# One core, attention and MLP: the scheduler's priorities replaced by an explicit sequence, and w_in loaded by column quarters

## The chip, the cores and the metric

The kernel runs on one core of a Trainium2 chip. The metric is the device time of one execution in microseconds (us), smaller is better. Executions of one kernel scatter by some 1%. "Before" is the kernel without the change, "the changed kernel" the one with it.

Engines: PE is TensorE (PEld its weight loads), DVE VectorE, ACT ScalarE, POOL GpSimd, SP SyncE, which here only issues DMAs.

## The reference, cut to what matters

Block-sparse attention (every query keeps the 6 best of 24 key chunks of 32, chosen by an upper bound), then an MLP with hard-swish:

```python
B, H, S, D = 4, 8, 768, 64
ub = sum(maximum(q * k_min, q * k_max))             # per query and chunk
top_chunks = argsort(ub)[..., -6:]                   # causal chunks only
scores = where(selected & causal, q @ k.T / 8, -1e9)
x = (softmax(scores) @ v) -> [3072, 512]
h = x @ w_in                                         # 512 -> 2048
out = (h * clip(h + 3, 0, 6) / 6) @ w_out            # 2048 -> 512
```

## The kernel before: the parts that the change and the argument touch

Two heads make a "pair"; there are 16 pairs, four to a batch. The kernel does not emit its instructions in source order. It first lists all its parts as `Op`s with an engine, a duration, a key (smaller is sooner), dependencies and ring buffers, then a list scheduler goes through them in modelled time and emits them. For a pair i the parts are, in the naming that I use throughout: k, q, v (loads), C (V cast on POOL), K and Q (transposes on PE, then copies and minima and maxima), R (Q copy in bf16 on POOL), U, V, L (bound, top 6, selection), S.0 to S.5 (score bins; exponential on ACT, mask on POOL), P (attention times V). For a group g of 384 tokens: X (transposes), H.0 to H.14 (eight groups of 8 matmuls, then ACT and DVE), O (output, in quarters of 4 matmuls). w0 to w3 load w_in, w4 to w7 w_out.

```python
def run(self, slack):
    ...                                        # cut: candidates, dependencies
            for eng, lst in cand.items():
                mine = None
                for op in lst:
                    if op.key is None:
                        op.key = front
                    r = self.ready(op)         # None while its ring buffer is in use
                    ...
                    if mine is None or (at + s < mine[0]) or (at < mine[0] + s and op.key < mine[1].key):
                        mine = (at, op)

rings = dict(big=3, sm=2, ks=3, qs=3, vb=3, vs=3, ...)       # buffers; big and sm are PSUM

s["ldk"] = add("LD", 2.07, i - 4.0, lambda: ld(s["ks"], k, "KS"), take=[s["ks"]], chain="ldk")
s["ldq"] = add("LD", 2.07, i - 3.9, lambda: ld(s["qs"], q, "QS"), take=[s["qs"]], chain="ldq")

for kt in range(KT_HID):                       # w_in by row blocks, issued from POOL (they cast to bf16)
    iss = add("POOL", 0.6, 0.3 + 0.05 * kt,
              lambda kt=kt: nc.gpsimd.dma_start(WIN[:, kt, :], moe_w_in[kt * P:(kt + 1) * P, :]),
              deps=[st[2 + kt // 2]["o_v"]], chain="wi")
    res.append(add("LD", 3.1, 0.01 * kt, None, deps=[iss], chain="w"))

ORDER = "K3 S0 L1 P0 Q3 S1 P1 S2 U2 S3 V2 S4 S5".split()     # one pair's keys; the MLP gets a pace
```

The plan models DMA: one lane "LD", one load after the other by key, and the weights (`None` as their function) in the same lane. On the chip the weight loads go through a queue of their own (q0 in the DMA views below) and land some 8 us after POOL issues them (median 8.6 us for w_in, 8.0 for w_out).

The softmax here doesn't subtract the row's maximum and nothing guards it: scores larger than these inputs give would overflow.

## Time and profile before

| | before |
|---|---|
| time | 320.94 us, median of 3 runs (320.07 to 321.49) |
| span of the profiled execution | 321.6 us (that execution took 323.29 us) |
| PE busy | 296.4 us, 92% |
| DVE, ACT, POOL busy | 174.0, 178.9, 76.8 us |
| chain of waits | 85% PE |
| first H matmul | 67.4 us |

From the page of the kernel before: busy time, then the granted PE clock and the DMA rate in 40 slices of 8 us.

```profile
PE 296.4 (92%) x2976; PEld 177.1 (55%) x2992; DVE 174.0 (54%) x464; ACT 178.9 (56%) x217; POOL 76.8 (24%) x149
...
PEclk9769977999999999999999999999999999999999
DMA  9998999997606144361401200000011001100101
GB/s 211 265 242 177 211 202 202 195 229 171 147 9 141 67 101 113 82 153 30 101 34 67 49 2 35 33 35 2 2 45 56 0 3 65 35 0 35 65 33 65
```

The reader is to see three things. PE is the busiest engine by far. The clock is granted below full speed only in the first seven slices. And DMA is busy for 70% or more of each of the first ten slices, partly used in the next ten, and nearly idle after that.

From the chain of waits of the kernel before (start, duration, engine, tile, line), up to L of pair 3:

```profile
34.54 0.56 DVE Xb L462
35.10 0.88 DVE KM L283
35.97 0.02 issue
36.00 0.81 ACT LHS L298
36.80 0.02 issue
36.83 0.96 DVE KC_122 L283
37.79 0.10 DVE RINV L457
37.89 0.74 DVE QP L313
38.62 0.71 DVE KC_122 L291
39.34 1.08 DVE T_654 L362 x12
40.41 0.46 DVE Xb L462
40.87 0.38 DVE SEL_127 L365
41.24 0.05 issue
41.29 0.30 PE SLT L382 x3
```

Here the chain leaves PE for 7 us. It does so again ahead of the next two L (47.8 to 51.5 and 55.8 to 60.5 us), for 3.7 and 4.8 us. What PE waits for is the selection, which stands behind other work in DVE's order. This is what a better order can shorten.

The loads of Q for pair 7 in the kernel before (all DMAs that write QS in 46 to 52 us):

```profile
L243 SPq DMA_DIRECT2D QS<-in_q_dram x2: 627/1823/3019, 46.6 to 49.7; - x2
...
DMA to landing us min/median/max: 8.7/9.9/11.1
```

PE used them at 65.8 us, just ahead of its first five H groups:

```profile
65.81 0.83 PE L273 MATMUL QT<-IDENT_111,QS 128*128 128x128 f32 x6
...
67.44 6.67 PE L514 MATMUL HP<-XT,WIN 128*128 128x384 bf16 x40
```

### The profile page before, as it was taken

To read this page: it belongs to the slowest core of one execution; us is meant where nothing else is said; L and a number is where in the kernel's file an instruction comes from. 1 tells how busy PE (TensorE), PEld (TensorE's weight loads), DVE (VectorE), ACT (ScalarE), POOL (GpSimd) and SP (SyncE) were. 2 spreads that over 40 slices of the span, in tenths; PEclk is the share of its full clock that TensorE was granted. 3 is DMA by queue.
4 is the path that set the end of the run, shared out by engine and by line. 5 is a ranking of instruction groups with operands and counts; after the bars stand their busy time and mean duration, and the time that the engine had idled before them with its cause. 6 is when DMAs were issued, how large, how long until landed. Compare 5 with 4: busy or idle time off the path is not lost.

```text
span 321.6 us, 7243 instructions
## 1 busy us (share of the span) xinstructions
PE 296.4 (92%) x2976; PEld 177.1 (55%) x2992; DVE 174.0 (54%) x464; ACT 178.9 (56%) x217; POOL 76.8 (24%) x149
## 2 busy tenths in 40 slices
PE   3567888899999999999999999999999999999995
PEld 2345665666665464576546564566555555564542
DVE  7367955789786052478534683466522541471330
ACT  0428856866876154666656665586455862462431
POOL 7125654721431012140322122240211211000000
PEclk9769977999999999999999999999999999999999
DMA  9998999997606144361401200000011001100101
GB/s 211 265 242 177 211 202 202 195 229 171 147 9 141 67 101 113 82 153 30 101 34 67 49 2 35 33 35 2 2 45 56 0 3 65 35 0 35 65 33 65
DMA packets 81440, 29.82 MB, mean 93 GB/s; under 512 B 75776, under 2 KB 77824, under 8 KB 81408
## 3 DMA queue, kind: packets, MB, share of 16 engines
q1 hardware_dynamic: 77152, 24.78, 31.2%
q0 software_dynamic: 2688, 4.19, 7.7%
q10 hardware_dynamic: 1568, 0.39, 0.5%
q8 instruction: 23, 0.38, 0.5%
q14 instruction: 9, 0.07, 0.1%
HBM read 27.26 MB, written 6.29 MB: 104 GB/s over the span
## 4 chain that ended last, share of the span: by engine, by line
PE 85%; DVE 8%; ACT 4%; issue 1%; POOL 1%; POOLq 0%; ACTq 0%
PE HP L514 26%; PE OP L538 26%; PE SPS L412 7%; PE PVP L452 7%; PE SPS L417 5%; PE KT L273 4%; PE UBP L332 3%; PE QT L273 2%; PE XTP L494 2%; PE UBQ L354 2%; DVE KM L283 1%; ACT U L518 1%; PE SLT L382 1%; DVE EM L230 1%; ACT LHS L298 1%
## 5 line engine op out<-in xcount | busy, mean ns | idle before, releaser
L423 ACT ACTIVATE PT<-SPS 128x1024 bf16<-128x1024 f32 x96 | 85.3, 919 | 38.8 <-PE SPS L417 37.8
L514 PE MATMUL HP<-XT,WIN 128*128 128x384 bf16 x512 | 89.5, 326 | 1.2 <-DVE GT L524 1.2
L538 PE MATMUL OP<-WOUT,GT 128*128 128x512 bf16 x368 | 86.5, 380 | 1.5 <-issue 1.0
L524 DVE SCALAR_TENSOR_TENSOR GT<-U,HP 128x768 bf16<-128x768 bf16 x64 | 60.9, 952 | 40.0 <-ACT U L518 39.8
L518 ACT ACTIVATE U<-HP,THREE 128x768 bf16<-128x768 f32 x64 | 57.7, 901 | 37.9 <-PE HP L514 37.3
L427 POOL TENSOR_SCALAR_AFFINE_SELECT PT<-PT 128x256 bf16<-128x256 bf16 x96 | 39.1, 413 | 127.2 <-ACT PT L423 125.1
L514 PEld LDWEIGHTS <-WIN 128*128 128x128 bf16 x512 | 47.9, 98 | 33.0 <-issue 3.7
L538 PEld LDWEIGHTS <-GT 128*128 128x128 bf16 x384 | 35.2, 98 | 42.5 <-issue 4.0
L412 PE MATMUL SPS<-RHS,LHS 64*128 64x512 bf16 (+3 forms) x256 | 35.8, 318 | 2.5 <-ACT PT L423 1.9
L544 ACT ACTIVATE OT<-OP 128x512 f32<-128x512 f32 x24 | 14.3, 596 | 41.2 <-PE OP L538 39.0
L417 PE MATMUL SPS<-SELT,EM 64*128 64x288 bf16 (+6 forms) x384 | 33.4, 255 | 0.0
L452 PEld LDWEIGHTS <-PT 128*128 128x128 bf16 x672 | 24.8, 101 | 3.6 <-issue 2.0
L283 DVE TENSOR_REDUCE KM<-KT 128x24 f32<-128x768 f32 x16 | 15.3, 954 | 17.4 <-PE KT L273 17.0
L412 PEld LDWEIGHTS <-LHS 64*128 64x128 bf16 x256 | 11.4, 95 | 21.7 <-issue 18.3
L417 PEld LDWEIGHTS <-EM 64*128 64x128 bf16 x384 | 19.0, 97 | 7.8 <-issue 1.4
L319 POOL CAST RHS<-QTS 128x768 bf16<-128x768 f32 x16 | 14.7, 920 | 33.2 <-ACT QTS L309 28.3
L273 PE MATMUL KT<-IDENT_111,KS 128*128 128x128 f32 x96 | 16.2, 313 | 4.2 <-DMA KS<-in_k_dram 4.2
L298 ACT CAST LHS<-KT 128x768 bf16<-128x768 f32 x16 | 12.8, 799 | 12.0 <-DVE KM L283 8.6
L462 DVE TENSOR_TENSOR Xb<-PVP,RINV 128x384 bf16<-128x384 f32 x32 | 17.6, 554 | 0.8
L457 DVE RECIPROCAL RINV<-PVP 128x6 f32<-128x6 f32 x32 | 6.1, 192 | 22.0 <-PE PVP L452 21.9
L340 DVE TENSOR_TENSOR UBT<-UBP,BIAS 96x384 f32<-96x384 f32 x16 | 8.8, 549 | 16.1 <-PE UBP L332 16.1
L313 DVE TENSOR_SCALAR QP<-QTS 128x576 f32<-128x576 f32 x16 | 11.3, 705 | 10.0 <-ACT QTS L309 9.9
(103 smaller groups left out, 229.6 us busy)
## 6 DMA issues: line engine op xcount, KB each, us to landing
VS<-in_v_dram SPq DMA_DIRECT2D x32, 192.0 KB, 3.6
out_dram<-OT SPq DMA_DIRECT2D x24, 256.0 KB, 2.0
KS<-in_k_dram SPq DMA_DIRECT2D x31, 192.0 KB, 3.3
QS<-in_q_dram SPq DMA_DIRECT2D x31, 192.0 KB, 3.5
WIN<-in_moe_w_in_dram POOLq DMA_DIRECT2D x4, 512.0 KB, 8.6
WOUT<-in_moe_w_out_dram POOLq DMA_DIRECT2D x4, 512.0 KB, 8.0
KS<-in_k_dram ACTq DMA_DIRECT2D x1, 192.0 KB, 3.3
QS<-in_q_dram ACTq DMA_DIRECT2D x1, 192.0 KB, 4.4
```

The source lines that it names most:

```text
L273: nc.tensor.transpose(T[:, j * P:(j + 1) * P], src.obj[:, j].rearrange("p e d -> p (e d)"), IDENT32[:])
L283: nc.vector.tensor_reduce(out=dst, in_=kt.obj[:, 0:S].rearrange("p (c w) -> p c w", w=CH), axis=AX.X, op=op)
L412: nc.tensor.matmul(T[:, e, c:c + hi - lo], lhsT=s["lhs"].obj[e * D:(e + 1) * D, j * P:(j + 1) * P], rhs=s["rhs"].obj[e * D:(e + 1) * D, lo ...
L417: nc.tensor.matmul(T[:, e, c:c + hi - lo], lhsT=EM[e * D:(e + 1) * D, h, j * P:(j + 1) * P], rhs=s["selt"].obj[e * D:(e + 1) * D, x:x + hi ...
L423: nc.scalar.activation(T[:, :, 0:w], sp.obj[:, :, 0:w], ACT.Exp, scale=scale)
L427: nc.gpsimd.affine_select(out=dv, in_=dv, pattern=[[0, 2], [1, P]], compare_op=A.is_ge, fill=0.0, base=0, channel_multiplier=-1)
L452: nc.tensor.matmul(T[:, qb, :], lhsT=t[:, e, c:c + P], rhs=fx(s["vb"])[:, e, j, :], start=(j == 0), stop=(j == qb))
L462: nc.vector.tensor_tensor(out=xb[b].obj[:, :, h * D:(h + 1) * D], in0=pv.obj[:, :, 0:D], in1=s[("ri", e)][:].to_broadcast([P, NBLK, D]), o ...
L514: nc.tensor.matmul(T[:, f, 0:GRP], lhsT=WIN[:, kt, (f0 + f) * P:(f0 + f + 1) * P], rhs=xt.obj[:, kt, :], start=(kt == 0), stop=(kt == KT_H ...
L518: nc.scalar.activation(new(u, [P, 2, GRP], BF16, "U")[:], hp.obj[:, :, 0:GRP], ACT.Relu, bias=THREE[:], scale=1.0)
L524: nc.vector.scalar_tensor_tensor(out=gt.obj[:, f0:f0 + 2, :], in0=u.obj[:], scalar=6.0, in1=hp.obj[:, :, 0:GRP], op0=A.min, op1=A.mult)
L538: nc.tensor.matmul(T[:, :], lhsT=gt.obj[:, f, t * P:(t + 1) * P], rhs=WOUT[:, f, :], start=(f == 0), stop=(f == FT - 1))
```

## The change

Intent: take the order of all parts from one explicit sequence, found by annealing in the plan's own model, with durations set closer to the measured ones; and load w_in by column quarters, so that H.0 needs one quarter of it and not all.

```diff
-    def add(self, eng, dur, key, fn=None, deps=(), take=(), use=(), chain=None):
+    def add(self, eng, dur, tok, fn=None, deps=(), take=(), use=(), chain=None):
...
-        op = Op(eng, dur, key, fn, deps, take, use)
+        op = Op(eng, dur, tok, self.place(tok), fn, deps, take, use)
...
+SEQUENCE = """
+V0 S0.2 R0 K0 k2 q1 R3 w7 q0 S0.4 S0.1 U0 k3 v5 v0 R1 P0.0 v6 w4 S3.0 R2 S0.0 v1 S0.3 S0.5 V2 V4 k0 w0 k4 w6 Q3
...                                      (some 30 lines)
+POS = {tok: n for n, tok in enumerate(SEQUENCE.split())}
...
-        for kt in range(KT_HID):
-            iss = add("POOL", 0.6, 0.3 + 0.05 * kt,
-                      lambda kt=kt: nc.gpsimd.dma_start(WIN[:, kt, :], moe_w_in[kt * P:(kt + 1) * P, :]),
-                      deps=[st[2 + kt // 2]["o_v"]], chain="wi")
+        for n in range(4):
+            c = n * (DFF // 4)
+            iss = add("POOL", 0.63, f"w{n}",
+                      lambda c=c: nc.gpsimd.dma_start(WIN[:, :, c:c + DFF // 4], wi[:, :, c:c + DFF // 4]),
+                      deps=[st[WGATE[n]]["o_v"]], chain="wi")
...
-            o = add("PE", 1.30, kk, mm, deps=xts + wdma[:KT_HID], take=[hp], use=[xt], chain="H")
+            o = add("PE", 1.31, tok, mm, deps=xts + [wdma[f0 * 4 // FT]], take=[hp], use=[xt], chain="H")
...
-    ORDER = "K3 S0 L1 P0 Q3 S1 P1 S2 U2 S3 V2 S4 S5".split()
```

The order that PE gets around the first H (built, not run): `... S4.0 X0.0 U5 X0.2 U6 V5 H0.0 Q7 V6 L5 S4.1 H0.2 H0.4 ...`. Before, five H groups ran at the first opportunity and Q7 came just ahead of them.

## The prediction

> **What bounds the kernel now.** TensorE, but not evenly. The page gives PE 296.4 us busy of 321.6 (92%), the others 56% or less; the chain of waits is 85% PE. Priced from warm pieces of the chain: one H group (8 matmuls of 384) 1.30 us, an O quarter 0.86, a P 0.66, a K or Q transpose group 0.66, U 0.80, V 0.47, L 0.30, X 0.33, the S bins of a pair about 2.7. Times their counts, the program is about 281 us at full clock. About 40 us are lost:
>
> - Front. In the chain the first H matmul starts at 67.5 us. What ran before it (PE timeline: K, Q of pairs 0 to 7, U 0 to 6, V 0 to 5, S, P of 0 to 3) is an estimated 38 us of full-clock work, so about 30 us are lost. In the busy-by-stretch view PE is idle 11.6 us in 0-24 us and 6.2 us in 24-64, and the granted clock is 0.79, 0.62, 0.79, 0.79 in 8-16, 16-24, 40-48, 48-56. (The Trainium skill, "TensorE: Matmul & The Clock Gate", part 1, says an under-used PE is clocked at half rate in windows of about 3.4 us; the clock row agrees.) The chain there is not PE: from 34.3 to 41.2 and 47.8 to 51.5 us it runs through DVE and ACT (KM, KC, QP, T8, SEL), ending in SLTs that PE waited for, 0.7 to 1.3 us. A pair takes 9 to 10 us, while its work is some 7 us on each of PE, ACT and DVE.
> - Middle, 67.5 to 318 us: about 7 us, around H groups mixed with S and P (gaps near 97-103 and 178-186 us).
> - End: 3.5 us, the last output copy and store.
>
> **What the change does.** Same arithmetic; it only reorders. The built order keeps the first eight PE groups (K0 to U1) and the load order of pairs 0 to 8. Then: all six S0 bins in one run; K3 before P0 and U4, V4 before S3, so selection runs further ahead of the S that needs it; most of S4 before the first H; H in runs of mostly seven or eight; K7, K8, K9 put under O work; O5.2 between the last P and the last X's. Before the first H stands an estimated 37-38 us of PE work, as before, so an earlier first H is pure gain.
>
> w_in by column quarters: same bytes, 2 KB source rows instead of 8 KB. w_out's pieces already have 2 KB rows and land in 8.0 us against 8.6, so no cost. H then needs one quarter, but w_in wasn't the wait: first H follows P3 and X0 closely.
>
> **Sum.** Up to S0 at 20.5 us nothing changes. From there ACT (exponentials 1.02 us, copies 0.8) with three PSUM buffers sets the pace; walking the order I get S1 near 31, S2 near 39, first H at 59-63 instead of 67.5: 6 to 8 us gained. Middle: 2 to 5 us. End: 0. Predicted 310 us, range 302 to 317. Chances: faster by over 2% 0.73, within 2% 0.25, slower 0.02.
>
> **Right if:** first H near 61 us; PE idle after 24 us roughly halved; granted clock about 1.00 from 32 us on; PE busy falls to about 290; busy time of DVE, ACT, POOL unchanged; S0 still starts near 20.5.
>
> **Wrong if:** runs of S and K bunch on ACT or DVE, which work strictly in order, so that real waits exceed the plan's; faster consumption meets the DMA limit (about 200 GB/s throughout 0-72 us now) and K or Q loads come late; half clock moves elsewhere. More gain if the front reaches ACT's bound, first H near 55.

## The result, and the profile after

Ratios here and below are the mean time of one kernel's fast runs over the mean of the other's of the same rounds, so not quite the ratio of the medians that are quoted.

| | before | changed |
|---|---|---|
| median time | 321.19 us (4 runs) | 315.82 us (4 runs, 315.66 to 317.32) |
| ratio | | 0.985, 95% interval 0.9811 to 0.9888 |
| PE busy | 296.4 us | 292.0 us |
| span, profiled | 321.6 us | 314.1 us |
| first H | 67.4 us | 60.4 us |

So 1.5% faster, which counts as the same at a 2% line; 3.4% had been forecast. From the page of the changed kernel:

```profile
PE 292.0 (93%) x2992; PEld 178.4 (57%) x2992; DVE 173.8 (55%) x464; ACT 178.6 (57%) x217; POOL 78.1 (25%) x149
...
PEclk9979999979999999999999999999999999999999
DMA  9994999996402575550232000100011000000121
GB/s 210 279 262 86 221 219 212 218 257 140 102 16 66 138 182 129 146 136 1 49 88 53 0 33 35 69 33 2 0 35 68 2 35 35 33 0 3 44 89 67
```

The clock row is better than before in the front, but it has a new dent in the ninth slice. The DMA row has a hole in the fourth. The PE timeline of the changed kernel around the first H (start, us, engine, line, operation; in brackets the idle time ahead of it and what ended that):

```profile
60.01 0.54 PE L382 MATMUL UBQ<-IDENT_111,UBT 96*96 96x96 f32 x4
60.38 1.47 PE L537 MATMUL HP<-XT,WIN 128*128 128x384 bf16 x8
64.04 1.47 PE L301 MATMUL QT<-IDENT_111,QS 128*128 128x128 f32 x6 [2.19 <-DMA QS<-in_q_dram]
...
67.23 7.93 PE L537 MATMUL HP<-XT,WIN 128*128 128x384 bf16 x47
```

One H group starts at 60.38, as forecast. Then PE stands still for 2.19 us until the Q load of pair 7 has landed, and Q7 takes 1.47 us where the same group takes 0.82 at full clock. The run of H that matters starts at 67.23. Busy time by stretches of 4 us of the changed kernel (PE, PEld, DVE, ACT, POOL; clock; DMA share; GB/s):

```profile
56.00:60.00 4.00, 4.00 (x89) 2.60 (x85) 3.12 (x7) 3.62 (x5) 3.14 (x6) 1.00 1.22 203
60.00:64.00 4.00, 1.84 (x18) 1.06 (x12) 3.04 (x15) 0.90 (x1) 0.18 (x1) 1.00 1.13 239
64.00:68.00 4.00, 3.96 (x23) 2.85 (x24) 1.82 (x15) 1.40 (x2) 0.82 (x1) 0.57 1.17 265
```

The stall has a second price: the clock is granted at 0.57 on average in the 4 us behind it. And the loads concerned (all DMAs that write QS in 50 to 60 us):

```profile
L266 SPq DMA_DIRECT2D QS<-in_q_dram x2: 2368/2494/2620, 54.0 to 56.4; - x2
...
DMA to landing us min/median/max: 7.5/8.4/9.3
```

Issued at 54.0 and 56.4 us, 7 us later than before, and landed at 63.9. They were needed at 61.85, when H0.0 ends. Demand came 4 us earlier and the data 6 us later. The 7 us were already there one pair sooner: Q of pair 6 was issued at 42.35 us and not at 35.07, when the first w_out load had only just been issued (42.1). Ahead of it stand the hole and the second half of w_in, issued at 32.5 us and not at 39.3.

To see what is lost where, I split each profiled span at the first H:

| profiled kernel | first H at | span | from first H to the end |
|---|---|---|---|
| before | 67.4 | 321.6 | 254.2 |
| changed | 60.4 | 314.1 | 253.7 |
| changed, second (below) | 60.2 | 312.9 | 252.7 |

The front gained 7 us in this pair of profiles. The middle, from which 2 to 5 us were expected, gained half a microsecond, 1.5 in the second look. The cut isn't at equal work: by the counts of matmuls ahead of the first H (678 before, 665 changed), the changed order has one K, one Q, one X and one L group fewer there and one score bin more. At the prediction's prices that is some 1.5 us (an estimate) that moved from the front to the middle.

### The profile page after: what moved, and what is told of

Same layout as the page of the kernel before. It is cut to its first block, busy times and chain, and to the rows that moved or that the text cites. A ratio compares the mean times of both kernels' runs of the same rounds, so it can differ in the third digit from the quotient of the medians.

```text
span 314.1 us, 7230 instructions
## 1 busy us (share of the span) xinstructions
PE 292.0 (93%) x2992; PEld 178.4 (57%) x2992; DVE 173.8 (55%) x464; ACT 178.6 (57%) x217; POOL 78.1 (25%) x149
## 4 chain that ended last, share of the span: by engine, by line
PE 87%; DVE 5%; ACT 3%; DMA 2%; POOL 1%; issue 1%; SPq 0%; ACTq 0%; POOLq 0%
PE OP L561 27%; PE HP L537 26%; PE PVP L480 7%; PE SPS L440 7%; PE SPS L445 5%; PE UBP L360 4%; PE KT L301 3%; PE QT L301 3%; DMA QS<-in_q_dram 2%; PE UBQ L382 2%; PE XTP L517 2%; ACT PT L451 1%; DVE KM L311 1%; PE SLT L410 1%; DVE EM L253 1%
## 5 line engine op out<-in xcount | busy, mean ns | idle before, releaser
L451 ACT ACTIVATE PT<-SPS 128x1024 bf16<-128x1024 f32 (+1 forms) x96 | 83.1, 924 | 21.8 <-PE SPS L445 19.6
L561 PE MATMUL OP<-WOUT,GT 128*128 128x512 bf16 x384 | 88.9, 379 | 0.0
L537 PE MATMUL HP<-XT,WIN 128*128 128x384 bf16 x512 | 85.9, 326 | 0.0
L537 PEld LDWEIGHTS <-WIN 128*128 128x128 bf16 x512 | 49.5, 98 | 32.1 <-issue 0.7
L445 PE MATMUL SPS<-SELT,EM 64*128 64x288 bf16 (+6 forms) x384 | 32.4, 252 | 0.0
L347 POOL CAST RHS<-QTS 128x768 bf16<-128x768 f32 x16 | 15.7, 984 | 40.7 <-ACT QTS L337 39.5
L480 PEld LDWEIGHTS <-PT 128*128 128x128 bf16 x672 | 23.4, 97 | 2.8 <-issue 1.0
L440 PEld LDWEIGHTS <-LHS 64*128 64x128 bf16 x256 | 11.3, 95 | 14.0 <-issue 10.8
L301 PE MATMUL KT<-IDENT_111,KS 128*128 128x128 f32 x96 | 14.6, 296 | 4.6 <-DMA KS<-in_k_dram 4.2
L301 PE MATMUL QT<-IDENT_111,QS 128*128 128x128 f32 x96 | 15.2, 304 | 2.6 <-DMA QS<-in_q_dram 2.2
L337 ACT COPY QTS<-QT 128x768 f32<-128x768 f32 x16 | 12.6, 804 | 5.6 <-PE QT L301 5.5
```

The source lines that it names most:

```text
L301: nc.tensor.transpose(T[:, j * P:(j + 1) * P], src.obj[:, j].rearrange("p e d -> p (e d)"), IDENT32[:])
L440: nc.tensor.matmul(T[:, e, c:c + hi - lo], lhsT=s["lhs"].obj[e * D:(e + 1) * D, j * P:(j + 1) * P], rhs=s["rhs"].obj[e * D:(e + 1) * D, lo ...
L445: nc.tensor.matmul(T[:, e, c:c + hi - lo], lhsT=EM[e * D:(e + 1) * D, h, j * P:(j + 1) * P], rhs=s["selt"].obj[e * D:(e + 1) * D, x:x + hi ...
L451: nc.scalar.activation(T[:, :, 0:w], sp.obj[:, :, 0:w], ACT.Exp, scale=scale)
L480: nc.tensor.matmul(T[:, qb, :], lhsT=t[:, e, c:c + P], rhs=fx(s["vb"])[:, e, j, :], start=(j == 0), stop=(j == qb))
L537: nc.tensor.matmul(T[:, f, 0:GRP], lhsT=WIN[:, kt, (f0 + f) * P:(f0 + f + 1) * P], rhs=xt.obj[:, kt, :], start=(kt == 0), stop=(kt == KT_H ...
```

## The experiments

Twelve runs were made. Where an experiment must move single instructions, the plan's order is kept for each engine, the named parts are moved, and the list is emitted again by a routine that asserts every dependency and every ring buffer; the edits are then one or two lines. All twelve gave the right result. Each was profiled in one execution.

**Theories.** S: the forecast is right but for one load, Q of pair 7, which stops PE right after the first H. Under S there are two causes to separate. H: the fourth slice's hole in DMA (the run of S0 bins puts K2 at 26 us instead of 21, so pair 5's loads wait for a buffer). W: the weight loads, issued some 5 us earlier than before, take the DMA from the Q, K and V loads. Rivals: C, something later absorbs the stall, so that removing it gives nothing; D, lateness is general; N, the stall was an accident of one execution.

### The changed kernel again

No edit.

> A second look at the changed kernel. Theory S (a single late load spoils the front): PE again waits 2 us or more for QS of pair 7 just after the first H group (near 62 us), and the clock is granted at half for about 3.4 us there; time 315 to 317. Rival N (that stall was an accident of one execution): no such wait in this profile, and the time is the same anyway.

Measured: 315.19 us (314.36 to 317.08), ratio 0.9813 (0.9756 to 0.987). PE again waited 2.7 us for QS of pair 7, at 61.6 to 64.4:

```profile
64.37 0.85 PE L301 MATMUL QT<-IDENT,QS 128*128 128x128 f32 x6 [2.74 <-DMA QS<-in_q_dram]
```

In this execution the clock did not fall behind it (from first H to the end 252.7 us instead of 253.7). PE had also waited 0.55 us for a Q6 load. The half clock that was expected at this place did not come. N falls. The stall is a feature of the order; the half clock behind it comes in some executions only.

### One more buffer for each loaded tensor

```diff
-            pools[r] = ctx.enter_context(tc.tile_pool(name="p_" + r, bufs=n))
+            pools[r] = ctx.enter_context(tc.tile_pool(name="p_" + r, bufs=n + (r in ("ks", "qs", "vs"))))
```

> One more buffer each for the loaded K, Q and V; every engine's order is unchanged. Theory S with cause H (the run of S0 bins moved K2 from 21 to 26 us, so the fifth pair's loads wait for a buffer, DMA stands idle for 5 us at 23 to 28, and as DMA then runs full until 74 us those 5 us reach Q7): the hole goes, QS of pair 7 lands about 5 us earlier (59 or before), PE does not wait near 62 us, time about 312 (3 to 4 us less than the changed kernel). Rival W (the weight loads' share of DMA is what makes Q7 late, the hole is harmless): QS still lands after 61.9 and the time stays within 1 us of the changed kernel. Rival C (a later limit absorbs the stall): the stall goes, time stays near 315.8.

Measured: 313.66 us (311.89 to 313.98), ratio 0.973 (0.9679 to 0.9782). The hole is filled, and Q7 is as late as ever. First the stretch of the hole and a PE line of the deeper buffers, then the same stretch of the changed kernel:

```profile
24.00:28.00 4.00, 3.37 (x40) 2.62 (x37) 2.98 (x10) 3.31 (x5) 3.49 (x6) 1.00 0.96 211
...
63.75 0.85 PE L301 MATMUL QT<-IDENT,QS 128*128 128x128 f32 x6 [2.35 <-DMA QS<-in_q_dram]
```

```profile
24.00:28.00 4.00, 3.40 (x38) 2.66 (x35) 3.13 (x16) 3.31 (x5) 3.46 (x7) 1.00 0.05 13
```

DMA moved 211 GB/s there instead of 13, and still QS landed at 63.7, PE waited 2.35 us. Q of pair 6 was issued 4.6 us sooner (37.7 us), Q of pair 7 only 0.8 sooner (53.1): what was won ahead of the w_out loads was lost beside them. So H is not the cause of the stall, against my first expectation. The time, though, fits neither theory. The median is 1.5 us below that of the changed kernel on the same chip, where W had said within 1 us, and all four runs lie below all four of the changed kernel. The two profiles from first H to the end differ by 0.3 us only (252.4 and 252.7), and the intervals of the ratios overlap. If the gain is real, it came with the stall in place, and its cause is open.

### The w_out loads later

```diff
+    move(eng["POOL"], ("w4", "w5", "w6", "w7"), "R8")    # behind R7: 65 to 68 us instead of 42 to 54
```

> The four w_out loads are issued after R7 on POOL (near 66 us instead of 42 to 53); all else keeps its order. Theory W or H: with 2 MB less in front of it, QS of pair 7 lands several us earlier, no PE wait near 62 us, time about 312, unless the first O group (near 85 us) now waits for w_out. Rival C: stall gone, time near 315.8.

Measured: 312.72 us (312.0 to 313.99), ratio 0.9732 (0.9681 to 0.9783). No PE wait for QS is left, and Q7 follows H0.0 at once. PE timeline with late w_out:

```profile
60.45 1.47 PE L586 MATMUL HP<-XT,WIN 128*128 128x384 bf16 x8
61.75 0.82 PE L350 MATMUL QT<-IDENT,QS 128*128 128x128 f32 x6
63.59 7.96 PE L586 MATMUL HP<-XT,WIN 128*128 128x384 bf16 x48
```

The first H is where it was (60.45), the long H run starts 3.6 us earlier, and from first H to the end it takes 249.9 us instead of 252.7 to 253.7. Why: the Q loads of pair 7 with late w_out (all DMAs that write QS in 48.5 to 51 us), and the DMA queues in 48 to 60 us (packets, MB, share of 16 engines' time), first of the changed kernel, then with late w_out. q1 carries the Q, K and V loads, q0 the weights.

```profile
L315 SPq DMA_DIRECT2D QS<-in_q_dram x2: 644/755/866, 49.0 to 49.7; - x2
...
DMA to landing us min/median/max: 4.6/4.6/4.6
```

```profile
q0 software_dynamic: 1413, 1.41, 73.5%
q1 hardware_dynamic: 4199, 1.06, 44.7%
```

```profile
q1 hardware_dynamic: 11448, 2.87, 106.7%
```

Of the 2.47 MB that DMA moved in these 12 us, the weights had 1.41. Without them the loads moved 2.87 MB in the same time and landed in 3.4 to 4.6 us after their issue instead of 7.5 to 9.3 (the Q loads issued in 48 to 56 us and in 50 to 60 us). Q of pair 7 was also issued 5 us sooner, at 49.0 us, and landed at 54.3 instead of 63.9. The Trainium skill, "DMA: Bandwidth & Descriptors", section "Queues, rings and completion order", says that each DMA engine takes turns between the queues that have work, a whole packet at a time; its packet typically holds some 9 to 17 descriptors. What the profile counts as packets is 1.0 KB for weights and 0.25 KB for Q here. Whether these are the page's packets isn't shown, and turns of one for one don't come out of the counts (1413 against 4199). What is shown is the share of bytes.

This confirms W for the w_out loads: without them in the way, Q7 is in time though the hole stays (98 GB/s in the fourth slice). It refutes C. By time alone it isn't told from deeper buffers (313.66 us), and its interval overlaps that of the changed kernel; the four runs lie below the changed kernel's four, and the way from first H to the end, 2.5 us shorter than with deeper buffers, tells them apart.

### Q7 later, loads untouched

```diff
+    for e in ("PE", "ACT", "DVE"):
+        move(eng[e], ("Q7",), "H0.12")
+    move(eng["POOL"], ("R7",), "R8")
```

> Loads as in the changed kernel; only the Q7 group (PE, ACT, DVE, POOL) is moved behind H0.10, so that PE has 6 H groups and S4.1 to do while QS is on its way. Theory S: PE does not wait near 62 us, the clock stays full, time about 312, as with the loads mended. Rival D (being late is general, not one load): other K, Q or V groups then wait for DMA and most of the gain is lost.

Measured: 313.0 us (312.57 to 314.89), ratio 0.9722 (0.9679 to 0.9765). With the loads as late as they were, PE has H groups to do meanwhile, and the wait for Q7 is gone; from first H to the end 250.4 us. In its profile PE also waited 1.0 us for a Q6 load, half clock fell at 38 us, and its first H came at 62.9; D is right in this small part. Mending the consumer gives what mending the load gives, so in the way from first H to the end it is the stall that cost the time, and not anything else that late w_out might change.

### w_in by rows again, in the new order

```diff
-                      lambda c=c: nc.gpsimd.dma_start(WIN[:, :, c:c + DFF // 4], wi[:, :, c:c + DFF // 4]),
+                      lambda n=n: nc.gpsimd.dma_start(WIN[:, n, :], moe_w_in[n * P:(n + 1) * P, :]),
...
+    for op in order:                       # each H now needs all four loads
+        if op.eng == "PE" and op.tok[0] == "H":
+            op.deps += [w for w in wdma[:4] if w not in op.deps]
```

> The changed kernel with w_in loaded by row blocks again, every order kept (each H then waits for all four loads). If the column quarters cost or gain nothing (as the prediction said), time within 1 us of the changed kernel (315 to 316), QS of pair 7 late again near 64 us. If their 2 KB rows are what takes the DMA from Q and K, WIN lands sooner, QS lands several us earlier, and the time is near 312.

Measured: 316.0 us (315.04 to 317.41), ratio 0.9792 (0.9743 to 0.9842), the changed kernel's 0.9813 within its interval. The stall is there (2.8 us), with half clock behind it, and one K load was 1.6 us late besides. The quarters are neither cause nor gain.

### The quarters alone, in the old order

```diff
-                      lambda kt=kt: nc.gpsimd.dma_start(WIN[:, kt, :], moe_w_in[kt * P:(kt + 1) * P, :]),
+                      lambda c=kt * (DFF // 4): nc.gpsimd.dma_start(WIN[:, :, c:c + DFF // 4], wi[:, :, c:c + DFF // 4]),
```

> The kernel before with w_in loaded by column quarters and nothing else. Both theories of the reorder: same as before within 0.5% (its w_in is there long before the first H). If quarters alone slow the other loads, 1% slower.

Measured: 321.29 us (320.03 to 322.97), ratio 0.9984 (0.9928 to 1.004): nothing, as expected. The profile gave something else. The order is that of before, but the clock was granted at half less often in the front, and the first H came at 64.2 us, not 67.4. My base for the front was an unlucky execution. So was the spare time: here Q of pair 7 landed near 59.3 us for a use at 62.5, with 3 us to spare and not 7.

### Late w_out in the old order (control)

```diff
+    late = [op for op in lst if "plan_weights" in op.fn.__qualname__][4:]   # the four w_out loads on POOL
+    ...                                                                     # go behind the eighth RHS copy
```

> Control: the kernel before with its four w_out loads issued behind the eighth RHS copy (near 67 us). Theory W with slack (before has the same contention, but needs Q7 4 us later and has it 6 us sooner): no gain, within 0.5% of before. If late w_out is a gain for any order, 1% faster, and then it says nothing on why the change gave less.

Measured: 321.77 us (319.96 to 321.84), ratio 0.9963 (0.9908 to 1.0018). Late w_out is no gain by itself; it only helps where the order needs the loads sooner. Before has much the same contention (1.21 MB of weights and 1.14 MB of loads in 48 to 60 us); it has the slack to bear it. First H at 65.9, from there to the end 254.2.

### Late w_out and deeper buffers together

Both edits, run on two chips.

> The changed kernel with late w_out loads and with one more buffer each for K, Q and V. Theory W (only the weights' share matters, once K, Q and V are there in time more buffers give nothing): the same as late w_out alone, about 312.7. If the idle DMA at 24 to 28 us costs something by itself (the deep buffers took about 1.5 us off without ending the Q7 wait): about 311.

> The combination again, beside its next variant on one chip. The same as the first time: 0.967 of before, no PE wait for a Q load, first H near 60 us.

Measured: 311.55 us (311.49 to 312.01), ratio 0.9668 (0.9622 to 0.9714), and 313.01 us (311.95 to 313.91), ratio 0.9741 (0.9704 to 0.9778). From first H to the end 249.9 and 249.8 us, as with late w_out alone. The second missed its expectation of 0.967, which lies below its interval. Whether the deeper buffers add anything on top stays open; the two runs of the same kernel differ by as much.

### An early table load, which first went wrong

ACT loads its function table in 1.28 us at 8.1 us, in the chain before the first LHS. A one-column Exp at the start takes it out of there:

```diff
         nc.vector.memset(THREE[:], 3.0)
+        nc.scalar.activation(const.tile([P, 1], FP32, name="WARM")[:], THREE[:], ACT.Exp)
```

> The combination, with a one-column Exp on ACT in the first microseconds so that its table load (1.28 us, at 8.1 us in the chain before LHS of the first pair) is done before it is needed. If the first 20 us are a chain of latencies, as the prediction said, and everything after keeps its pace: S0 starts about 1.3 us earlier (near 19.6 instead of 20.9), time about 310.3. If DMA or the clock sets the pace of the front instead: S0 earlier, but first H still near 60 and the time within 0.3 us of the combination.

Measured: 314.3 us (314.01 to 314.71), ratio 0.9781 (0.9753 to 0.9809), slower than the combination on the same chip by 1.3 us, where 310.3 us had been expected. S0 came earlier (19.8 us), but PE waited 1.8 us for a K load near 44 us: the loads ran slower from the start (174 GB/s in the first 8 us, 205 in the combination). The new tile is 4 bytes per partition and lies ahead of the load buffers. Two more runs separate the tile from the table load:

```diff
-        nc.scalar.activation(const.tile([P, 1], FP32, name="WARM")[:], THREE[:], ACT.Exp)
+        nc.scalar.activation(const.tile([P, 64], FP32, name="WARM")[:, 0:1], THREE[:], ACT.Exp)
```

> The early table load again, its scratch now 256 bytes per partition instead of 4. Theory L (the 4 bytes moved the load buffers[...], which cut the Q, K, V loads from 280 to 217 GB/s): 280 GB/s again at 8 to 16 us, no late K5, S0 about 1.2 us earlier than in the combination, time about 310.5. Rival T (the early table load itself, or this chip, slows the loads): 217 GB/s again and the time near 314.

```diff
-        nc.scalar.activation(const.tile([P, 1], FP32, name="WARM")[:], THREE[:], ACT.Exp)
+        nc.vector.memset(const.tile([P, 1], FP32, name="WARM")[:], 3.0)
```

> The combination with a 4-byte tile more in front of the load buffers and no early table load. Theory L: loads at 217 GB/s in 8 to 16 us, K5 late, time 314 or more. Rival T: loads at 280 GB/s, time near 312 to 313.

Measured: with 256 bytes 311.71 us (310.81 to 312.74), ratio 0.9689 (0.9646 to 0.9732). With the 4-byte tile and no early table load 313.84 and 312.25 us in its two fast runs, 318.03 and 318.25 in two that were slow, so no ratio; theory L had said 314 or more, which the two fast runs do not reach. The stretch of 8 to 16 us, in which only Q, K and V loads run, decides. In turn the combination, the 256-byte scratch, the 4-byte tile alone:

```profile
8.00:16.00 8.00, 4.17 (x40) 3.10 (x40) 2.74 (x13) 3.31 (x4) 1.12 (x1) 1.00 1.24 281
```

```profile
8.00:16.00 8.00, 4.28 (x40) 3.22 (x40) 4.02 (x18) 3.00 (x4) 1.37 (x2) 1.00 1.22 275
```

```profile
8.00:16.00 8.00, 4.89 (x43) 3.42 (x41) 2.74 (x11) 3.15 (x4) 1.95 (x2) 1.00 1.39 218
```

281, 275 and 218 GB/s: the 4 bytes cost the loads over a fifth of their rate, on two chips, with or without the table load (218 GB/s with both). The runs without the small tile had 258 to 281 in this stretch, so 275 is within their spread. So in the rate of the loads theory L holds against T: it is the size of the tile ahead of the buffers, not what ACT does. With the scratch at 256 bytes S0 starts at 19.2 us instead of 20.5, the first H at 59.3, and the ratio lies between the two of the combination (0.9668 and 0.9741), so the time doesn't tell whether the early table load pays.

## Why the prediction was wrong

**Right.** The first H was forecast at 59 to 63 us; it came at 60.4, 60.2 and 61.3 in the three profiles of the new order with unmended loads. S0 started at 20.9 us (20.5 forecast). Busy times of DVE, ACT and POOL stayed. The column quarters cost and gave nothing (0.9984 alone). The middle did gain by the prediction's own cut: once Q7 is in time, the way from first H to the end takes 249.8 to 249.9 us (late w_out, and the combination twice) against 254.1 to 254.2 (before, quarters alone, control). That is 4.3 us, inside the 2 to 5 forecast. That it falls inside is in part the cut: with the 1.5 us of work that moved behind the first H, the estimate at equal work is nearer 6 for the middle and 4 for the front.

**The step that failed.** "Before the first H stands an estimated 37-38 us of PE work, as before, so an earlier first H is pure gain." It wasn't. Some 1.5 us of the earlier first H is work that moved behind it (the estimate above), and the rest was in part lost again. The first H came early and PE then stood still in the group behind it, for 2.2, 2.7 and 2.8 us in the three profiles, with half clock after it in two of them. This took back 2.8 to 3.9 us of the middle's gain in the two profiles of the changed kernel (252.7 and 253.7 against 249.85), as late w_out and a later Q7 show when they remove the stall. My own list of what could go wrong had it ("faster consumption meets the DMA limit ... and K or Q loads come late"), but the sum gave it no microseconds, because before no PE wait for a later load shows. A wait that isn't there says nothing about how much is to spare. It could be read from before's trace: Q of pair 7 landed near 58 us for a use at 65.8, and the changed order wanted it 4 us sooner. That it would also be issued 7 us later could not be read from there.

**A second term was mis-sized.** I priced the front from one profile, with the first H at 67.4 us. Two kernels with the same order of matmuls had it at 64.2 and 65.9. The clock rows explain the direction: before has four slices well below full clock in its front (second, third, sixth, seventh), the control three, the quarters alone one, and the first H comes in that order. The mean of the three is 65.8, so the front gained some 5.6 us (to 60.3, the mean of the two profiles of the changed kernel) and not 7. That the profiled execution was 2 us above the median (323.29 against 320.94) was in front of me.

**Also wrong.** "Granted clock about 1.00 from 32 us on" failed in the first profile (0.57 at 64 to 68). "PE idle after 24 us roughly halved": 13.6 us before (25.2 in all, 11.6 of it to 24 us), 10.8 after. The "DMA limit (about 200 GB/s ...)" is no limit: before itself moved 264 GB/s in 8 to 16 us, when only Q, K and V were loading. And my first explanation on seeing the result, the hole in DMA, fell: filled, it left the stall as it was.

**The sum.** Forecast 10.9 us: about 7 front and 4 middle. Measured 5.4 in the medians, 5.5 less. The stall (2.8 to 3.9) and the front's base (1.4) make 4.2 to 5.3 of that. With the stall removed in two independent ways 312.7 and 313.0, and 311.6 and 313.0 with deeper buffers: 8 to 11 us below before's medians of the same rounds. These versions beat both kernels; their ratios of 0.967 to 0.974 stand beside the 0.966 that 310 us would have been.

**Why did annealing not see it?** Argued, not shown: the plan holds one DMA lane in which a weight load waits its turn by key, so w4 to w7, with late places, cost Q7 nothing there. On the chip they start at their issue. The traces show the second half of this (w4 issued at 42.1 us, w_out bytes moving in 48 to 60 us beside Q7's); I did not re-anneal with a corrected model.

## What to carry to other kernels

Before a reordering, list for each load the time between landing and first use, in several executions, and not only the waits: the spare time is what the new order consumes. Here loads issued early, off the critical path, still took bandwidth from those that were on it (1.06 MB beside them, 2.87 MB without), so issue bulk weights as late as their use allows. And price a stage from several profiled executions when the clock varies in it.

## What the Trainium skill lacked or had wrong

- "DMA: Bandwidth & Descriptors", section "How a descriptor splits into AXI transactions", tells that a start off a 256-byte boundary costs extra beats, but gives no measured rate, and "SBUF — State Buffer", section "Operand start alignment", says that its runs timed nothing. Here a 4-byte tile ahead of the load buffers cut loads made of 256-byte pieces from 281 to 218 GB/s, and 256 bytes in its place gave 275. (I infer that the buffers' addresses moved; no view shows addresses.)
- "DMA: Bandwidth & Descriptors", section "Queues, rings and completion order", doesn't say how little is left for small packets beside large ones: 1.06 MB in 12 us beside weight loads, 2.87 MB without them.
- "TensorE: Matmul & The Clock Gate", part 1, ties half clock to at least one idle window of about 3.4 us. Here 2.2 us of PE standing still was followed by it in one execution (0.57 at 64 to 68 us; in the 3.41 us ahead of the fall PE had been busy for 1.21), and 2.7 us wasn't in another.
